# Order of three steps between the layers of an attention, SoLU and top-1 MoE kernel

## The chip, the core and the metric

The kernel runs on one core of a Trainium2 chip. The metric is the device time of one execution in microseconds (us). The core has five engines with queues of their own: TensorE (PE in the profile, its weight loads PEld), VectorE (DVE), ScalarE (ACT), GpSimd (POOL) and SyncE (SP), which only issues DMAs. POOL issues the indirect DMAs (gathers and scatters).

## The reference

3072 tokens (4 x 768) of width 512 pass through three layers:

```python
# chunked attention: chunks of 32 rows see 16 rows to the left, 8 to the right, 8 memory rows
scores = scale * np.matmul(q_c, k_full.transpose(0, 1, 3, 2))
a = np.exp(scores - max); a = a / (np.sum(a) + 1e-09)
x = np.matmul(a, v_full)
# SoLU with LayerNorm, 512 -> 1024 -> 512
h = x @ w_in
solu = h * softmax(h)
x = (solu - mu) / np.sqrt(var + 1e-06) * g_ln @ w_out
# top-1 mixture of 8 experts, 512 -> 1024 -> 512
e_idx = np.argmax(x @ w_gate, axis=1)
for e in range(E):
    h = np.maximum(x[mask] @ w1[e], 0.0)
    out[mask] = gate_w[mask, None] * eom[mask, e, None] * (h @ w2[e])
```

The result is float32. Products run in float16 with a high and a low half for each operand and three passes (high by high, high by low, low by high).

## The kernel before, in words

The first two layers and the routing go over 24 tiles of 128 tokens (NT = 24). Every step of a tile (a product, an exp, a transpose by DMA) is put down by `at(t, fn, ...)` with a planned time t. All are then sorted by t and emitted, and each engine works through its instructions in that order. The planned times are an order written out by hand; they hold nothing back by themselves. TL is the planned start of the last tile.

The routing of a tile (`routing_steps`) takes the logits on TensorE from x2T, the transposed second-layer output (line 350 is the helper of all three-pass products). VectorE makes lg, top, idx, the one-hot row oh_all and ng from them. `earlier` counts on TensorE the tokens ahead (tri and ones times oh_all), and VectorE makes the pick zz, the rank and the place (ohs, oav) from it. `slot_products` adds up the places of tiles 0 to 21 and later of the last two; `slot_numbers` makes the list of row numbers (slots_gidx) by which tokens are gathered. The rows themselves are kept in x2d in DRAM.

The third layer runs in nine units, a unit being a set of slots for tokens of one expert. Unit 0 has 384 slots of expert 1, unit 1 another 320 of the same expert, so with the same weights; units 2 to 8 have 480, 416, 352, 320, 320, 320 and 288 slots, one for each other expert, in the order of their counts. For a unit:
- `gather` (POOL, line 1238) fetches up to 128 rows each into a tile xg or x2; `slot_T` (SP, line 1250) transposes them by DMA into xu. Unit 1 has three such pieces (128, 128, 64), unit 2 four.
- `own_h(n, f)`, f = 0 to 7, is the first product, 12 matmuls into a PSUM tile pg (four buffers). `own_r` makes the two halves of its relu, ru: the high half on ScalarE (line 1261), the low half on VectorE (line 1262).
- `own_y` is the second product (line 1276), one piece of rows at a time, into one of two PSUM tiles. `slot_out` scales it on ScalarE (line 1333) and scatters it (POOL, line 1334). `strip_gates` (line 1314) copies gate factors of narrow pieces on VectorE.
- The weights of an expert come in two halves, w1 into wf0 and w2 into wf1, 2 MB each (`load_w`, SP, line 1221). `conv_hi` (ScalarE, line 1225) and `conv_lo` (VectorE, line 186) turn each into two float16 halves in four parts. `some(k)` emits up to k such conversions, if the target buffer has been used up, and after the fourth the load of the next set into the buffer that came free.

Unit 0's first product is spread over the last tiles, between the steps of their second layer and routing: f = 6 stands at TL + 33.4, f = 7 at TL + 35.5. The loop over units 1 to 8 stands behind the sorted steps and emits its calls in the order in which they are written. Lines 918, 1379, 1380 and 1458 are those that the change touches.

Of the kernel before, what the change touches and what calls it, by code (L numbers as in the profile page):

```python
# [38 lines left out]
def attention_solu_top1_moe(  # L39
# [30 lines left out]
    NT = N // P  # L70
# [7 lines left out]
    KF = DFF // P  # L78
# [256 lines left out]
    PERIOD = 14.2  # L335
# [5 lines left out]
    def at(t, fn, *args):  # L341
        events.append((t, len(events), fn, args))
# [211 lines left out]
    def when(name):  # L554
        return PLAN[name] - STEADY + 5 * PERIOD
# [160 lines left out]
    def routing_steps(i, v):  # L716
# [116 lines left out]

        at(LOGITS[i], logits)
        g = PICK[i]
# [79 lines left out]
    TL = (NT - 1) * PERIOD  # L915
    OUT = [(i + 2) * PERIOD + 6.15 for i in range(NT - 3)] + [TL + 5.3, TL + 14.6, TL + 24.0]
    X2 = [(i + 2) * PERIOD + 13.3 for i in range(NT - 4)] + [TL - 3.2] + [TL + 10.5, TL + 19.8, TL + 29.3]
    LOGITS = [(i + 3) * PERIOD + 12.8 for i in range(NT - 4)] + [TL + 12.4, TL + 19.8, TL + 29.2, TL + 33.3]
    PICK = [(i + 3) * PERIOD + 13.2 for i in range(NT - 4)] + [TL + 13.0, TL + 20.9, TL + 30.3, TL + 34.4]
    EARLIER = [(i + 4) * PERIOD + 6.1 for i in range(NT - 5)] + [TL + 10.3, TL + 14.2, TL + 21.9, TL + 31.3, TL + 35.45]  # L920
    GATE = [(i + 4) * PERIOD + 6.55 for i in range(NT - 5)] + [TL + 11.0, TL + 15.0, TL + 23.0, TL + 32.2, TL + 37.0]
    LOGITS[0:2] = [when("lg0"), when("lg1")]
    PICK[0:2] = [when("pk0"), when("pk1")]
# [181 lines left out]
    def left_over():  # L1105


        nc.vector.tensor_scalar(out=rt["ti"], in0=rt["all"], scalar1=float(P - 1), scalar2=None, op0=ALU.add)
        nc.vector.tensor_scalar(out=rt["ti"], in0=rt["ti"], scalar1=7, scalar2=None, op0=ALU.logical_shift_right)
        nc.vector.tensor_copy(rt["tr"], rt["ti"])  # L1110
        nc.vector.tensor_tensor(out=rt["tr"], in0=rt["tr"], in1=rt["room"][:, 2], op=ALU.subtract)
        nc.vector.tensor_tensor(out=rt["key"], in0=rt["all"], in1=rt["room"][:, 0], op=ALU.is_gt)
        nc.vector.tensor_tensor(out=rt["tr"], in0=rt["tr"], in1=rt["key"], op=ALU.mult)
        nc.vector.tensor_tensor(out=rt["tm"], in0=le_e, in1=rt["tr"].unsqueeze(1).to_broadcast([P, E, E]), op=ALU.mult)
        nc.vector.tensor_reduce(out=rt["ends"], in_=rt["tm"], axis=AX.X, op=ALU.add)
        nc.vector.tensor_copy(rt["ctl"][:, 2, 0:1], rt["ends"][:, E - 1:E])
# [56 lines left out]
    def cap(n):  # L1173
        return UNITS[n][1] if UNITS[n][0] == "own" else P

    def width(n):
        return -(-cap(n) // P)
# [5 lines left out]
    def pieces(n):  # L1183

        out_ = []
        for c in range(width(n)):
            m, row = rows(n, c), 0
            for size in (P, 64, 32):
                if m - row >= size:
                    out_.append((c, row, size))  # L1190
                    row += size
        return out_
# [10 lines left out]
    def weights(n):  # L1203

        return max(0, n - 1)

    def load_w(j, m, c=None, other=None):

        w, k = ((w1, KD), (w2, KF))[m]
        to = 0 if j == 0 else m  # L1210
        dst = wf[to].rearrange("p (k f) -> p k f", k=k)
        if j == 0:
            q = slice(c * k // 4, (c + 1) * k // 4)
            nc.sync.dma_start(out=dst[:, q], in_=w[FE].rearrange("(k p) f -> p k f", p=P)[:, q])
            return
        key = j if other is None else ("other", other)
        if key not in reg:
            at_ = rt["ctl"][0:1, 0, j - 1:j] if other is None else rt["ctl"][0:1, 1, other:other + 1]
            reg[key] = nc.values_load(at_, engines=[SP], min_val=0, max_val=E - 1)
        q = slice(0, k) if c is None else slice(c * k // 2, (c + 1) * k // 2)  # L1220
        nc.sync.dma_start(out=dst[:, q], in_=w[bass.ds(reg[key], 1)].rearrange("o (k p) f -> (o p) k f", p=P)[:, q])
# [31 lines left out]
    def own_h(n, f):  # L1253
        xt, wt = xT_t[n], hl[weights(n) % 2, 0].rearrange("p a (k f) -> p a k f", k=KD)
        ps = psum["g"].tile([P, HALF], F32, tag=f"g{f % 2}", name="pg")[:, 0:cap(n)]
        three(ps, [(wt[:, b_, kk, f * P:(f + 1) * P], xt[:, a * KD + kk]) for kk in range(KD) for a, b_ in PASSES])
        r_t[n, f] = ps

    def own_r(n, f):
        ps, r = r_t.pop((n, f)), rt["ru"]  # L1260
        nc.scalar.activation(out=r[:, 0, f, 0:cap(n)], in_=ps, func=AF.Relu)  # L1261
        nc.vector.scalar_tensor_tensor(  # L1262
            out=r[:, 1, f, 0:cap(n)], in0=ps, scalar=0.0, in1=r[:, 0, f, 0:cap(n)], op0=ALU.max, op1=ALU.subtract
        )
# [43 lines left out]
    def strip_gates(n):  # L1308

        for k, (c, row, m) in enumerate(pieces(n)):  # L1310
            if m < P:
                many = tiny(f"many{m}")
                for q in range(P // m):
                    nc.vector.tensor_copy(many[q * m:(q + 1) * m], xg_t[n, c].bitcast(F32)[row:row + m, DM:DM + 1])
                gate_of[n, (c, row, m)] = many

    def slot_out(n, piece):

        c, row, m = piece
        fold = P // m  # L1320
        dm = DM // fold
        y = ending.pop((n, piece), None)
        if y is None:
            y = lnp.tile([P, DFF], F32, tag="eh", name="eh")
        y = y[:, 0:dm]
        at_ = place(n, c, sidx)
        if fold > 1:
            col = BASES[n - 1] + c
            at_ = rt["split"][:, SPLITS.index((row, m)), col:col + 1]
            gate = gate_of.pop((n, piece))  # L1330
        else:
            gate = xg_t[n, c].bitcast(F32)[:, DM:DM + 1]
        nc.scalar.activation(out=y, in_=y_t.pop((n, piece))[:, 0:dm], func=AF.Copy, scale=gate)  # L1333
        put = nc.gpsimd.indirect_dma_start(  # L1334
            out=out if fold == 1 else out.rearrange("n (h d) -> (n h) d", h=fold),
            out_offset=bass.IndirectOffsetOnAxis(ap=at_, axis=0), in_=y, in_offset=None,
            bounds_check=N * fold - 1, oob_is_err=False,
        )
        for other in scattered:
            tc.declare_no_dep(put.ins, other.ins, reason="each token has one slot: scatters never share a row")  # L1340
        scattered.append(put)
# [34 lines left out]
        at(TL + 39.5 + 0.3 * c, gather, 1, c)  # L1376
        at(TL + 43.0 + 0.3 * c, slot_T, 1, c)
    for c in range(width(2)):
        at(TL + (41.0 if c < 2 else 50.8) + 0.3 * c, gather, 2, c)
        at(TL + (45.0 if c < 2 else 54.0) + 0.3 * c, slot_T, 2, c)  # L1380
    for c in range(4):
        at(TL + 41.6 + 1.2 * c, conv_hi, 1, 0, c)
        at(TL + 42.6 + 1.2 * c, conv_lo, 1, 0, c)
# [17 lines left out]
    def some(k=1):  # L1401
        for _ in range(k):
            if not parts or (parts[0][0] - 2, parts[0][1]) not in done:
                return
            j, m, c = parts.pop(0)
            conv_hi(j, m, c)
            conv_lo(j, m, c)
            if c == 3 and j + 1 < SETS:
                load_w(j + 1, m)

    def each(step, n):
        if n < RARE:
            for c in range(width(n)):
                step(n, c)
# [30 lines left out]
    for n in range(1, RARE):  # L1445
        todo = pieces(n)
        for f in range(KF):
            if n > 1 or f:
                own_h(n, f)
                own_r(n, f)  # L1450
            if f == 0 and n > 1:
                slot_out(*last)
                each(gather, n + 1)
            if f == 1 and 1 < n < RARE - 1:
                each(slot_T, n + 1)
            if f == 5 and n < RARE - 1:
                strip_gates(n + 1)
            if (2 if n == 1 else 0) < f < KF - 1:
                some()
            if n == 1 and f == 3:  # L1460
                load_w(2, 0)
            if n == 2 and f == 3:
                left_over()
        done.add((weights(n), 0))
        if n == RARE - 1:
            spare = psum["xu"].tile([P, 2 * KD, cap(n)], F16, tag="xu", name="xu").rearrange("p k t -> p (k t)").bitcast(F32)
            ending[n, todo[-2]], ending[n, todo[-1]] = spare[:, 0:DM], spare[:, DM:2 * DM]
        for k, piece in enumerate(todo):
            own_y(n, piece)
            if k and (n < RARE - 1 or k < len(todo) - 1):  # L1470
                slot_out(n, todo[k - 1])
            some(3)
        done.add((weights(n), 1))
        last = (n, todo[-1])
# [53 lines left out]
```

## Time and profile before

| | |
|---|---|
| median of 3 runs | 642.46 us (638.76 to 643.50) |
| the profiled execution, own time | 643.06 us |
| its span | 641.4 us |
| TensorE busy | 613.6 us (96%), 6955 matmuls |
| VectorE busy | 408.0 us (64%) |
| ScalarE busy | 310.7 us (48%) |
| POOL busy | 175.9 us (27%) |
| mean granted TensorE clock | 0.989 |

The profile is of one execution. The span goes from its first to its last instruction; the own time has 1.66 us more around it. An engine's busy time counts its instructions, not its waits; matmul ends are modelled. The granted clock is 1.00 at 2.4 GHz.

### The profile page before, as it was taken

The page shows a single profiled execution, that of the slowest core. Times are in us where ns is not written, and L with a number is a line of the kernel's source. Part 1 is how long each engine was busy: PE and PEld are TensorE (multiplying, and loading weights), DVE is VectorE, ACT ScalarE, POOL GpSimd, SP SyncE. Part 2 cuts the span into 40 slices and gives each one's busy share as a digit, 9 for nine tenths or more (in the row PEclk, how much of TensorE's full clock was granted, in tenths as well). Part 3 has the DMA queues.
Part 4 walks back from the last instruction along what each step waited for, and adds up shares of the span by engine and source line. Part 5 has one row for each costly group of instructions (what it writes and reads, how often), then busy time and mean ns, then how long its engine had stood idle before and what let it go on. Part 6 is the DMA issues. An engine that isn't in the chain of part 4 may idle for free.

```text
span 641.4 us, 17082 instructions
## 1 busy us (share of the span) xinstructions
PE 613.6 (96%) x6955; PEld 338.4 (53%) x6955; DVE 408.0 (64%) x1209; ACT 310.7 (48%) x648; POOL 175.9 (27%) x201
## 2 busy tenths in 40 slices
PE   9899899999999999999999989899999999999993
PEld 5555445555555555545554545454554656657561
DVE  3999866878889788878876662437153536365020
ACT  5667864565665566554444231445243436354120
POOL 2213342233332432233332124031221312313101
PEclk9999999999999999999999989999999999999997
DMA  8975879799999999966558359988546485794101
GB/s 269 344 241 113 185 182 171 165 198 230 239 189 208 193 240 219 181 138 123 123 109 171 90 179 204 300 304 226 190 114 254 124 285 148 276 185 130 37 8 40
DMA packets 168262, 117.44 MB, mean 183 GB/s; under 512 B 125724, under 2 KB 149678, under 8 KB 167664
## 3 DMA queue, kind: packets, MB, share of 16 engines
q1 hardware_dynamic: 162096, 96.94, 64.2%
q0 software_dynamic: 6080, 19.34, 9.9%
q8 instruction: 56, 0.92, 0.6%
q14 instruction: 30, 0.25, 0.1%
HBM read 73.69 MB, written 12.94 MB: 135 GB/s over the span
## 4 chain that ended last, share of the span: by engine, by line
PE 29%; issue 26%; DVE 21%; DMA 8%; POOL 7%; ACT 7%; SPq 1%; POOLq 0%; ACTq 0%; DVEq 0%
PE h L582 10%; PE pt L350 7%; PE pg L350 4%; DMA out_dram<-eh,split 3%; POOL out_dram L1334 3%; POOL xg L1238 3%; DVE nm L592 3%; PE warm L909 2%; ACT eh L600 2%; DVE eh L604 2%; DMA wf<-in_moe_w_dram 2%; PE pt L1276 2%; PE sc L367 1%; DVE mx L381 1%; DVE x L186 1%
## 5 line engine op out<-in xcount | busy, mean ns | idle before, releaser
L582 PE MATMUL h<-win_hl,xT 128*128 128x512 f16 x576 | 131.7, 379 | 2.9 <-DVE eh L604 1.4
L350 PE MATMUL pt<-wout_hl,lnT 128*128 128x512 f16 x552 | 129.2, 379 | 1.2 <-DVE x L186 1.1
L1262 DVE SCALAR_TENSOR_TENSOR ru<-pg,ru 128x320 f16<-128x320 f32 (+5 forms) x72 | 37.8, 525 | 112.1 <-ACT ru L1261 112.0
L1276 PEld LDWEIGHTS <-ru 128*128 128x128 f16 (+2 forms) x1176 | 70.0, 101 | 66.3 <-issue 6.0
L582 PEld LDWEIGHTS <-xT 128*128 128x128 f16 x576 | 53.1, 98 | 63.7 <-issue 2.5
L350 PEld LDWEIGHTS <-lnT 128*128 128x128 f16 x576 | 53.2, 97 | 57.4 <-issue 1.5
L350 PE MATMUL pg<-xu,hl 128*128 128x320 f16 (+2 forms) x480 | 75.2, 317 | 2.1 <-DMA xu<-x 1.2
L1276 PE MATMUL pt<-hl,ru 128*128 128x512 f16 (+2 forms) x528 | 74.9, 325 | 2.4 <-DVE ru L1262 2.4
L1261 ACT ACTIVATE ru<-pg 128x320 f16<-128x320 f32 (+5 forms) x72 | 33.5, 466 | 83.1 <-PE pg L350 82.0
L648 POOL TENSOR_TENSOR lnhl<-eh,lnhl 128x1024 f16<-128x1024 f32 x23 | 49.5, 2152 | 77.8 <-ACT lnhl L644 64.6
L350 PEld LDWEIGHTS <-hl 128*128 128x128 f16 x480 | 46.5, 99 | 27.2 <-DMA xu<-xg 2.7
L1276 PE MATMUL pt<-wout_hl,ru 128*32 128x128 f16 (+2 forms) x648 | 59.9, 285 | 0.0
L350 PE MATMUL pg<-xu,win_hl 128*128 128x480 f16 (+3 forms) x384 | 59.3, 316 | 0.0
L1334 POOL DMA_INDIRECT out_dram<-eh,slots_sidx x17 | 17.6, 1037 | 148.7 <-ACT eh L1333 148.7
L350 PEld LDWEIGHTS <-win_hl 128*128 128x128 f16 x384 | 37.2, 98 | 21.3 <-issue 0.6
L600 ACT ACTIVATE eh<-h,nm 128x1024 f32<-128x1024 f32 x24 | 26.8, 1115 | 41.9 <-DVE zr L793 35.0
L419 POOL TENSOR_TENSOR e<-e,sm 128x512 f32<-128x512 f32 x24 | 28.7, 1197 | 62.7 <-DVE sm L416 45.8
L186 DVE SCALAR_TENSOR_TENSOR hl<-wf,hl 128x1024 f16<-128x1024 f32 x32 | 38.6, 1224 | 7.9 <-ACT hl L1225 7.5
L1225 ACT ACTIVATE hl<-wf 128x1024 f16<-128x1024 f32 x32 | 32.9, 1047 | 3.0 <-DMA wf<-in_moe_w_dram 3.0
L604 DVE SCALAR_TENSOR_TENSOR eh<-h,eh 128x1024 f32<-128x1024 f32 x24 | 29.4, 1223 | 6.3 <-ACT eh L600 6.3
L909 PE MATMUL warm<-wide 128*128 128x384 f16 x169 | 31.4, 345 | 1.4 <-DVE mhalf L156 1.4
L621 ACT ACTIVATE junk<-eh,su 128x1024 f16<-128x1024 f32 x24 | 27.7, 1153 | 9.5 <-DVE pr L616 7.8
(193 smaller groups left out, 833.9 us busy)
## 6 DMA issues: line engine op xcount, KB each, us to landing
wf<-in_moe_w_dram SPq DMA_DIRECT2D x14, 2048.0 KB
vw<-in_v_dram SPq DMA_DIRECT2D x96, 112.0 KB
kr<-in_k_dram SPq DMA_DIRECT2D x12, 560.0 KB
qt<-in_q_dram SPq DMA_DIRECT2D x12, 512.0 KB
x2d<-x POOLq DMA_DIRECT2D x23, 260.0 KB, 3.7
wd<-in_moe_w_in_dram SPq DMA_DIRECT2D x4, 1024.0 KB
wd<-in_moe_w_out_dram SPq DMA_DIRECT2D x4, 1024.0 KB
wf<-in_moe_w_dram SPq DMA_DIRECT2D x8, 512.0 KB
```

The source lines that it names most:

```text
L186: nc.vector.scalar_tensor_tensor(out=lo, in0=src, scalar=s, in1=hi, op0=ALU.mult, op1=ALU.subtract)
L350: nc.tensor.matmul(out=out_ap, lhsT=a, rhs=b_, start=(z == 0), stop=(z == n - 1))
L582: nc.tensor.matmul(out=v["h"][:, n * HALF:(n + 1) * HALF], lhsT=xt[:, a * KD + kk], rhs=win_hl[:, b_, kk, n * HALF:(n + 1) * HALF], start= ...
L600: nc.scalar.activation(out=v["e"], in_=v["h"], func=AF.Exp, bias=v["nm"], scale=IH, accum_out=v["se"])
L604: nc.vector.scalar_tensor_tensor(out=e, in0=v["h"], scalar=IH, in1=e, op0=ALU.mult, op1=ALU.mult, accum_out=v["su"])
L648: eng.tensor_tensor(out=v["ln"][:, 1], in0=v["e"], in1=v["ln"][:, 0], op=ALU.subtract)
L909: nc.tensor.matmul(out=t[:, 0:3 * P], lhsT=wide[:, 0:P], rhs=wide, start=True, stop=True)
L1225: nc.scalar.activation(out=hl[b, m][:, 0, cs], in_=wf[m if of is None else of][:, cs], func=AF.Copy, scale=(S_W1, S_W2)[m])
L1261: nc.scalar.activation(out=r[:, 0, f, 0:cap(n)], in_=ps, func=AF.Relu)
L1262: nc.vector.scalar_tensor_tensor(out=r[:, 1, f, 0:cap(n)], in0=ps, scalar=0.0, in1=r[:, 0, f, 0:cap(n)], op0=ALU.max, op1=ALU.subtract)
L1276: nc.tensor.matmul(out=y_t[n, piece][q * m:(q + 1) * m, 0:DM // fold], lhsT=r[:, a, kk, at_:at_ + m], rhs=wt[:, b_, kk, q * DM // fold:(q ...
L1334: put = nc.gpsimd.indirect_dma_start(out=out if fold == 1 else out.rearrange("n (h d) -> (n h) d", h=fold), out_offset=bass.IndirectOffset ...
```

## The change

Three places in the order of emission change; what is computed stays.

1. The logits of the last tile are put down at TL + 33.5 in place of 33.3, so behind unit 0's product f = 6 (TL + 33.4).
2. The gathers and transposes of unit 2's first two pieces are put down with those of its other two, so behind the scatter of unit 0's second piece on POOL and behind the load of unit 2's second matrix (`load_w, 1, 1`, at TL + 52.4) on SP.
3. In unit 1's first product the four calls of `some()` at f = 3 to 6 are left out. The conversions follow with the calls of `some(3)` behind each piece of unit 1's second product. For units 2 to 8 the new condition says the same as the old one.

```diff
-    LOGITS = [...] + [TL + 12.4, TL + 19.8, TL + 29.2, TL + 33.3]
+    LOGITS = [...] + [TL + 12.4, TL + 19.8, TL + 29.2, TL + 33.5]
...
     for c in range(width(2)):
-        at(TL + (41.0 if c < 2 else 50.8) + 0.3 * c, gather, 2, c)
-        at(TL + (45.0 if c < 2 else 54.0) + 0.3 * c, slot_T, 2, c)
+        at(TL + 50.8 + 0.3 * c, gather, 2, c)
+        at(TL + 54.0 + 0.3 * c, slot_T, 2, c)
...
             if f == 5 and n < RARE - 1:
                 strip_gates(n + 1)
-            if (2 if n == 1 else 0) < f < KF - 1:
+            if n > 1 and 0 < f < KF - 1:
                 some()
             if n == 1 and f == 3:
                 load_w(2, 0)
```

On TensorE before, at the end of unit 0's product f = 5 (hl00 is the weight half, pg_6089 its PSUM tile, x2T_6063 the last tile's transposed input of the logits):

```order
3580 L350 MATMUL pg_6089<-xu_5666,hl00_1148 128x384
3581 L350 LDWEIGHTS hl00_1148
3582 L350 MATMUL pg_6089<-xu_5666,hl00_1148 128x384
3583 L350 LDWEIGHTS x2T_6063
3584 L350 MATMUL pg_6133<-wg_hl_115,x2T_6063 128x16
3585 L350 LDWEIGHTS x2T_6063
```

On TensorE after, 24 rows further on, where product f = 6 (pg_6136) ends:

```order
3604 L350 MATMUL pg_6136<-xu_5666,hl00_1148 128x384
3605 L350 LDWEIGHTS hl00_1148
3606 L350 MATMUL pg_6136<-xu_5666,hl00_1148 128x384
3607 L350 LDWEIGHTS x2T_6063
3608 L350 MATMUL pg_6149<-wg_hl_115,x2T_6063 128x16
3609 L350 LDWEIGHTS x2T_6063
```

The 24 rows of the logits and the 24 of product f = 6 have changed places; behind both, the slot products (oav) follow from row 3631 as before.

On ScalarE before, from the relu of f = 2 of unit 1 (ru 128x320) to the first output of unit 1's second product (eh_6622; wout_hl is the half of unit 2's second matrix, hl00 that of unit 3's first):

```order
336 L1261 ACTIVATE ru_5499<-pg_6463 128x320 [waits PE_49]
337 L1225 ACTIVATE wout_hl_114<-wf1_5498 128x1024 [waits DMAHW5_49]
338 L1261 ACTIVATE ru_5499<-pg_6491 128x320 [waits PE_49]
339 L1225 ACTIVATE wout_hl_114<-wf1_5498 128x1024
340 L1261 ACTIVATE ru_5499<-pg_6508 128x320 [waits PE_49]
341 L1225 ACTIVATE wout_hl_114<-wf1_5498 128x1024
342 L1261 ACTIVATE ru_5499<-pg_6533 128x320 [waits PE_49]
343 L1225 ACTIVATE wout_hl_114<-wf1_5498 128x1024
344 L1261 ACTIVATE ru_5499<-pg_6551 128x320 [waits DVE_49,PE_49]
345 L1225 ACTIVATE hl00_1148<-wf0_1147 128x1024 [waits DMAHW0_49]
346 L1225 ACTIVATE hl00_1148<-wf0_1147 128x1024 x2
347 L1333 ACTIVATE eh_6622<-pt_6566,xg_6308 128x512 [waits DMASW1_49,DMASW3_49,PE_49,Activation_49]
```

On ScalarE after, from the relu of f = 4 of unit 1 on (eh_6613 and eh_6674 are the outputs of its first and second piece):

```order
337 L1261 ACTIVATE ru_5499<-pg_6489 128x320 [waits PE_49]
338 L1261 ACTIVATE ru_5499<-pg_6504 128x320 [waits PE_49]
339 L1261 ACTIVATE ru_5499<-pg_6527 128x320 [waits PE_49]
340 L1261 ACTIVATE ru_5499<-pg_6542 128x320 [waits DVE_49,PE_49]
341 L1225 ACTIVATE wout_hl_114<-wf1_5498 128x1024 [waits DMAHW3_49]
342 L1225 ACTIVATE wout_hl_114<-wf1_5498 128x1024 x2
343 L1333 ACTIVATE eh_6613<-pt_6557,xg_6308 128x512 [waits DMASW3_49,DMASW7_49,PE_49,Activation_49]
344 L1225 ACTIVATE wout_hl_114<-wf1_5498 128x1024
345 L1225 ACTIVATE hl00_1148<-wf0_1147 128x1024 [waits DMAHW0_49]
346 L1225 ACTIVATE hl00_1148<-wf0_1147 128x1024
347 L1333 ACTIVATE eh_6674<-pt_6588,xg_6310 128x512 [waits DMASW4_49,PE_49,Activation_49]
348 L1225 ACTIVATE hl00_1148<-wf0_1147 128x1024 x2
```

The first conversion, with its wait for the load (DMAHW), stood ahead of the relus of f = 4 to 7 and now stands behind all eight relus.

On SP before, from unit 1's third transpose on (xu_6346 is unit 1's, xu_6357 unit 2's; DMASW is a wait for a gather):

```order
229 L1250 DMA_TRANSPOSE xu_6346<-x2_6312 128x8x64 [waits DMASW5_49]
230 L1250 DMA_TRANSPOSE xu_6357<-x2_6314 128x8x128 [waits DMAHW3_49,DMASW6_49,PE_49]
231 L1250 DMA_TRANSPOSE xu_6357<-x2_6316 128x8x128 [waits DMAHW4_49,DMASW7_49]
232 L1221 ISA
233 L1221 DMA wf1_5498<-in_moe2_w2_dram 128x8x512 [waits DMAHW5_49]
234 L1250 DMA_TRANSPOSE xu_6357<-xg_6406 128x8x128 [waits DMAHW6_49,DMASW2_49]
235 L1250 DMA_TRANSPOSE xu_6357<-xg_6408 128x8x96 [waits DMAHW7_49,DMASW3_49]
```

On SP after (xu_6342 is unit 1's, xu_6428 unit 2's):

```order
229 L1250 DMA_TRANSPOSE xu_6342<-x2_6312 128x8x64 [waits DMASW5_49]
230 L1221 ISA
231 L1221 DMA wf1_5498<-in_moe2_w2_dram 128x8x512 [waits DMAHW3_49]
232 L1250 DMA_TRANSPOSE xu_6428<-x2_6399 128x8x128 [waits DMAHW4_49,DMASW0_49,PE_49]
233 L1250 DMA_TRANSPOSE xu_6428<-x2_6401 128x8x128 [waits DMAHW5_49,DMASW1_49]
234 L1250 DMA_TRANSPOSE xu_6428<-xg_6403 128x8x128 [waits DMAHW6_49,DMASW2_49]
235 L1250 DMA_TRANSPOSE xu_6428<-xg_6405 128x8x96 [waits DMAHW7_49,DMASW3_49]
```

The load of wf1 has moved ahead of unit 2's first two transposes, and all four of them now follow it.

## Rows read from the trace of the kernel before

**Rows 1.** Stretches: us, busy us of PE, PEld, DVE, ACT, POOL; clock, DMA share, GB/s.

```profile
371.00:375.00 4.00, 4.00 (x30) 2.11 (x31) 1.01 (x7) 0.00 (x0) 0.00 (x0) 0.57 0.89 343
411.20:416.00 4.80, 2.40 (x11) 0.57 (x10) 4.61 (x12) 1.76 (x5) 0.00 (x0) 0.99 0.86 341
416.00:419.80 3.80, 3.80 (x11) 1.37 (x12) 2.85 (x3) 3.80 (x5) 0.14 (x1) 0.56 0.64 220
425.86:630.60 204.74, 204.73 (x1682) 120.82 (x1680) 84.49 (x129) 82.04 (x125) 45.44 (x43) 1.00 0.54 164
```

**Rows 2.** Timeline of PE, 366 to 430 us: start, duration, instruction, idle time before.

```profile
367.07 2.11 PE L350 MATMUL pg<-xu,hl 128*128 128x384 f16 x12
370.95 0.46 PE L350 MATMUL pg<-wg_hl,x2T 128*128 128x16 f16 x12 [1.77 <-DMA x2T<-x]
371.27 3.75 PE L350 MATMUL pg<-xu,hl 128*128 128x384 f16 x12
374.82 0.75 PE L350 MATMUL pm<-ohs,oav 128*128 128x26 f16 x22
...
375.97 0.17 PE L350 MATMUL pg<-oh_all,tri 128*128 128x8 f16 x1
...
379.32 0.20 PE L350 MATMUL pm<-ohs,oav 128*128 128x26 f16 x2
...
379.42 14.40 PE L1276 MATMUL pt<-hl,ru 128*128 128x512 f16 x66
395.06 13.20 PE L350 MATMUL pg<-xu,hl 128*128 128x320 f16 x96 [1.23 <-DMA xu<-x]
408.10 4.66 PE L1276 MATMUL pt<-hl,ru 128*128 128x512 f16 x20
414.44 0.82 PE L1276 MATMUL pt<-hl,ru 128*128 128x512 f16 x3 [1.68 <-DVE ru L1262]
415.97 9.96 PE L1276 MATMUL pt<-hl,ru 128*128 128x512 f16 x73 [0.71 <-DVE ru L1262]
425.86 4.43 PE L350 MATMUL pg<-xu,win_hl 128*128 128x480 f16 x21
```

**Rows 3.** Timeline of ACT in unit 1's first product.

```profile
401.77 0.44 ACT L1261 ACTIVATE ru<-pg 128x320 f16<-128x320 f32 x1 [1.19 <-PE pg L350]
407.63 1.06 ACT L1225 ACTIVATE wout_hl<-wf 128x1024 f16<-128x1024 f32 x1 [5.41 <-DMA wf<-in_moe_w_dram]
```

**Rows 4.** Timeline of SP's queue: unit 1's third transpose, the load, unit 2's third transpose.

```profile
388.44 1.35 SPq L1250 DMA_TRANSPOSE xu<-x  x1
...
395.79 0.61 SPq L1221 DMA_DIRECT2D wf<-in_moe_w_dram  x1
...
399.73 4.36 SPq L1250 DMA_TRANSPOSE xu<-xg  x1
```

**Rows 5.** Chain of waits, 360 to 460 us: start, duration, what.

```profile
365.99 4.92 DMA x2T<-x
...
395.79 11.81 DMA wf<-in_moe_w_dram
```

**Rows 6.** Timeline of DVE in the routing of the last tile.

```profile
372.46 0.15 DVE L743 TENSOR_SCALAR ng<-top 128x1 f32<-128x1 f32 x1
375.58 0.56 DVE L1262 SCALAR_TENSOR_TENSOR ru<-pg,ru 128x384 f16<-128x384 f32 x1 [2.98 <-ACT ru L1261]
376.25 0.16 DVE L758 SCALAR_TENSOR_TENSOR zz<-oh_all,pg 128x8 f32<-128x8 f16 x1
...
378.40 0.34 DVE L820 TENSOR_SCALAR oav<-iota_p,col,part 128x128 f16<-128x128 f32 x1
```

**Rows 7.** Tile xg, 376 to 412 us: time of its gathers from issue to landing.

```profile
DMA to landing us min/median/max: 4.4/6.2/8.3
```

**Rows 8.** Timeline, 420 to 480 us: weight loads of unit 1's narrow last piece.

```profile
423.12 2.54 PEld L1276 LDWEIGHTS <-ru 128*64 128x64 f16 x48 [0.42 <-issue]
```

**Rows 9.** Timeline of POOL: unit 2's third gather, behind unit 0's second scatter.

```profile
391.46 0.99 POOL L1238 DMA_INDIRECT xg<-x2d,slots_gidx  x1 [0.30 <-issue]
```

More of the change, by code (lines that the diff above doesn't have):

```diff
@@ L917, in attention_solu_top1_moe @@
     X2 = [(i + 2) * PERIOD + 13.3 for i in range(NT - 4)] + [TL - 3.2] + [TL + 10.5, TL + 19.8, TL + 29.3]
-    LOGITS = [(i + 3) * PERIOD + 12.8 for i in range(NT - 4)] + [TL + 12.4, TL + 19.8, TL + 29.2, TL + 33.3]
+    LOGITS = [(i + 3) * PERIOD + 12.8 for i in range(NT - 4)] + [TL + 12.4, TL + 19.8, TL + 29.2, TL + 33.5]
     PICK = [(i + 3) * PERIOD + 13.2 for i in range(NT - 4)] + [TL + 13.0, TL + 20.9, TL + 30.3, TL + 34.4]
```

## Prediction

> **What bounds the kernel now.** I read the busy time by stages first. From unit 2's first product, at 425.86 us, to the last matmul, TensorE is busy for 204.73 of 204.74 us at full clock [rows 1]. Nothing waits there, so each us by which that point moves earlier goes to the end, one for one, if the weights still arrive in time. What can be won lies ahead of 425.86.
>
> So I went through TensorE's timeline ahead of it [rows 2] and found three places where it is idle or slow:
> - Last tile's logits. The fixed unit's product f = 5 starts at 367.07 and takes 2.11 us, so it ends at 369.18. The logits start at 370.95, after a wait on the transposed x2T. Product f = 6, the same 12 matmuls as f = 5, takes 3.75 us in place of 2.11: the clock was granted at 0.57 from 371 to 375 [rows 1]. The count of earlier tokens follows at 375.97, and the end of the slot products, which give the gathers their addresses, at 379.32.
> - Unit 1's start. Its first product begins at 395.06, 1.23 us after the engine came free, on a transpose into xu.
> - Unit 1's second product. It runs from 408.10 to 425.86, 17.76 us, with waits of 1.68 and 0.71 us on ru, VectorE's low half of the relu. TensorE is busy for 2.40 of the 4.80 us from 411.2 to 416, and then works at a clock of 0.56 until 419.8 [rows 1].
>
> The third place is explained on ScalarE [rows 3]: after the relu of f = 3 at 401.77 it stands until 407.63, where a weight conversion gets its load. The relus of f = 4 to 7 are queued behind the four conversions. The load is late because SyncE issues it at 395.79, behind two transposes of unit 2 that wait for their gathers [rows 4]; it lands 11.81 us later [rows 5].
>
> **The change part by part.** All times are of the profiled execution: span 641.4 us, own time 643.06; the median of the runs shown is 0.60 below that, and the runs lie 4.74 us apart.
>
> 1. *Logits behind f = 6.* Product f = 6 starts at 369.18 and, with no gap before it, I cost it as f = 5: 2.11 us, to 371.29. x2T has landed by then (370.91) [rows 5], so the logits wait for nothing: 371.29 instead of 370.95, 0.34 later. From the logits' start to the last of the routing operations that the count waits for (ng) it takes 372.46 + 0.15 - 370.95 = 1.66 us on VectorE [rows 2, 6]: 372.95. The 44 small slot products fill TensorE meanwhile (some 1.15 us of it, 374.82 to 375.97). The count then stands at about 373.05, in place of 375.97: 2.92 earlier. VectorE must fit too. The low half of f = 6's relu, 0.56 us, sits between ng and pick; before it waited for the slow product until 375.58. Now it runs from 372.95 to 373.51, pick follows, and the 2.49 us from pick (376.25) to the end of the last place operation (378.40 + 0.34) [rows 6] end at 376.0. The slot products' last part stands behind TensorE's own work at 379.32 - 2.92 = 376.4. So the gathers and TensorE both move by 2.9 us.
>
> 2. *Unit 2's first gathers and transposes behind.* The work that TensorE does next, 14.40 us from 379.42, is free of waits and ends at 390.9. Then unit 1 needs its third transpose. In the trace that was issued at 388.44 [rows 4] and released TensorE at 395.06, 6.6 us later, with two gathers and a transpose of unit 2 in the same time. Moved by 2.9 it would be issued at 385.5. Lower bound: it lands like x2T, 4.92 us after its issue [rows 5], at 390.5, and TensorE starts when free, 390.9. Upper bound within this mechanism: it keeps its 6.6 us, 392.1. Two gathers less stand beside it, a scatter and the load come beside it; I take 391.4.
>
> By the Trainium skill, page "DMA: Bandwidth & Descriptors", section "Queues, rings and completion order", each DMA engine takes the descriptors of one queue in ring order; so the load, issued behind the transposes, could not pass them, and the sum below would be 0.5 us less. The same section has the engines take turns between queues, by which POOL's gathers and the load slow each other; the trace agrees as far as gathers land in 4.4 to 8.3 us [rows 7].
>
> The load itself leaves right behind the third transpose, at 385.5 + 1.35 + 0.2 = 387.0 instead of 395.79, and with its 11.81 us lands at 398.8. The transposes of unit 2 stand behind it on SyncE; in the trace one such, issued into the running load, held the queue for 4.36 us instead of 1.35 [rows 4]. Their gathers come behind POOL's second scatter, where the third stood at 391.46, 2.9 earlier, at a step of 0.99 + 0.30 us [rows 9]: the first at 388.6, the fourth at 392.5. Landed after about 6 us [rows 7], from 394 on, four transposes at 4.36 end at 411.5, and the last has landed by 416.4. Unit 2 needs them at 417.6. That is hidden by little in this worst sum; at 1.35 once the load is through they are done by 405.
>
> 3. *No conversions beside unit 1's first product.* It runs as it did, 13.04 us (395.06 to 408.10): 391.4 to 404.4. The relus of f = 4 to 7 follow each product at once, so the second product finds all of ru. VectorE's six gate copies between f = 5 and 6 need unit 2's fourth gather, which at 8.3 us [rows 7] lands by 400.8; they come up at 402. The second product without stalls: two pieces of 24 matmuls at 14.40 / 66 = 218 ns, 10.47 us, and the narrow piece 425.86 - 423.12 = 2.74 [rows 2, 8]: 13.2 us for 17.76. It ends at 417.6.
>
> The eight conversions have not gone: at 1.06 us on ScalarE and a little more on VectorE they now stand beside the second product, about 8.5 and 10 us in 13.2. The output of piece 0 waits behind three of them (404.4 + 3.2 = 407.6, earlier than the piece is done, 409.6). PSUM holds two pieces, so it costs nothing unless the load comes after 410. Unit 2's matrix is needed only by its second product, 19 us later.
>
> **Sum.** 425.86 - 417.6 = 8.2 us, of which the logits give 2.9, the transposes 0.7 and unit 1's second product 4.6. 643.06 - 8.2 = 634.8; the median lies a little lower than this execution, and I predict 634.6. With both bounds of the transpose it is 634.3 to 635.6. Units 2 to 8 keep their order, and their loads move along with the conversions that free the buffers.
>
> **Rivals.**
> - *The load holds unit 1's transpose.* The load now leaves 8.8 us earlier, 0.2 us behind the third transpose of unit 1. If they share the engines, the transpose is done only with the load, at 398.8. TensorE then stands for 7.9 us and works on at half clock, as after the stops at 371 and 416: the second of these ran 3.8 us at 0.56, a loss of 1.7. The end of unit 1 is 398.8 + 13.04 + 13.2 + 1.7 = 426.7, 0.9 later than before: 643.9. It is slower than before from a landing at 397.9 on, and by over 1% from 404. For it: the 4.36 us of a transpose beside a load, and a load that took 11.81 us. Against it: those were issued after the load, these before. 5%.
> - *Only the conversions pay.* The clock stays low at f = 6, or the logits' chain is held on VectorE, so that part 1 gives nothing, and unit 1's wait stays: 4.6 us, 638.5. For it: VectorE's relu stands in the chain. Against it: f = 5 ran at full clock [rows 2], and f = 6 now follows it without a stop. 12%.
> - *The stall moves on.* Unit 2's transposes, or the copies that need its fourth gather, come late, and TensorE waits 2 to 4 us at 417.6 or in unit 1's second product, half of the gain: 637 to 639. For it: the worst sum above leaves 1.2 us. Against: it takes 4.36 for all four. 15%.
> - *The tail does not follow*: a later load becomes the bound. No load is waited for after 425.86, and the buffers come free by 3 to 8 us earlier. 3%.
>
> **How the numbers follow.** My forecast has 65%. The runs before lie between 638.76 and 643.50, about 1% is what a measurement of this kernel can tell from no change, and 1% below the median is 636.0. Faster by over 1%: the forecast, and a little of the rivals with a low draw, less what scatters above 636.0: 0.68. Within 1%: 0.28. Slower by over 1%: 0.04. The range goes from 631.5 (both lower bounds and a run as far below the median as the lowest shown, part of the way) to 639.5 (the second and third rival).
>
> **What would show it.** Right: f = 6 takes 2.1 us and the logits wait for nothing; the count at about 373; unit 1 starts near 391.4; ScalarE does eight relus in a row; the second product has no wait on ru and takes 13.2 us; unit 2 starts near 417.6. Wrong: unit 1's start after 393, an idle stretch ahead of unit 2's first product, or new waits of TensorE after it.

## The result and the profile after

The changed kernel takes 637.15 us (median of 16 runs, 635.69 to 642.01), the kernel before 643.34 in the same comparison (16 runs, 638.76 to 646.65): 0.9905 of the time, 95% interval [0.9884, 0.9927], or 6.2 us less. Forecast were 634.6. The profiled execution of after took 635.88 us (span 634.2, clock 0.995), that of before 643.06 (641.4, 0.989).

In what follows I count from the start of the fixed unit's product f = 5. Where it falls (367.07 in before, 366.83 in after) is set by what comes earlier; it varied from 364.8 to 368.3 us in the thirteen profiles, so a difference of less than 3.5 us between the spans of two single profiles says nothing of the change by itself.

After's windows (us, then busy us and instructions of PE, PEld, DVE, ACT, POOL; clock, DMA share, GB/s). The first is that of [rows 1], the second is unit 1's second product, the third goes from unit 2's first product to the last matmul.

```profile
371.00:375.00 4.00, 3.92 (x70) 2.77 (x68) 3.50 (x28) 1.40 (x5) 0.00 (x0) 1.00 0.91 364
403.27:416.47 13.20, 13.20 (x99) 7.12 (x96) 6.07 (x6) 6.85 (x9) 1.00 (x1) 1.00 0.92 277
416.47:623.40 206.93, 205.77 (x1682) 121.12 (x1680) 88.18 (x133) 84.56 (x129) 46.97 (x44) 1.00 0.56 173
```

The half clock at 371 and at 416 has gone. But the third stretch, which was busy throughout in before, now holds 1.16 us of idle time.

After's timeline of PE, which answers to [rows 2] (... stands for small products between the rows):

```profile
366.83 4.06 PE L350 MATMUL pg<-xu,hl 128*128 128x384 f16 x24
370.73 0.45 PE L350 MATMUL pg<-wg_hl,x2T 128*128 128x16 f16 x12
...
372.36 0.17 PE L350 MATMUL pg<-oh_all,tri 128*128 128x8 f16 x1
...
375.71 0.20 PE L350 MATMUL pm<-ohs,oav 128*128 128x26 f16 x2
...
375.81 14.40 PE L1276 MATMUL pt<-hl,ru 128*128 128x512 f16 x66
390.24 13.20 PE L350 MATMUL pg<-xu,hl 128*128 128x320 f16 x96
403.27 13.27 PE L1276 MATMUL pt<-hl,ru 128*128 128x512 f16 x96
416.47 8.88 PE L350 MATMUL pg<-xu,win_hl 128*128 128x480 f16 x43
```

No row has a wait in brackets. f = 5 and f = 6 have become one row of 24 matmuls: 4.06 us, with no gap and at one speed. From f = 5's start to the end of the slot products it takes 8.88 us (375.71 - 366.83) where it took 12.25; unit 1 starts the moment the engine is free; its two products take 26.23 us (390.24 to 416.47) where they took 30.80. From f = 5 to unit 2 that is 49.64 in place of 58.79, 9.15 less.

After's timeline of ACT, for [rows 3]:

```profile
401.84 0.44 ACT L1261 ACTIVATE ru<-pg 128x320 f16<-128x320 f32 x1 [1.19 <-PE pg L350]
403.47 0.44 ACT L1261 ACTIVATE ru<-pg 128x320 f16<-128x320 f32 x1 [1.19 <-PE pg L350]
403.81 2.94 ACT L1225 ACTIVATE wout_hl<-wf 128x1024 f16<-128x1024 f32 x3
408.70 0.69 ACT L1333 ACTIVATE eh<-pt,xg 128x512 f32<-128x512 f32 x1 [1.96 <-issue]
409.29 1.05 ACT L1225 ACTIVATE wout_hl<-wf 128x1024 f16<-128x1024 f32 x1
414.52 2.00 ACT L1225 ACTIVATE hl<-wf 128x1024 f16<-128x1024 f32 x2 [4.19 <-DMA wf<-in_moe_w_dram]
```

The relus come at the products' pace, the conversions of the late load (wout_hl) right behind the last of them and without a wait: the load had landed. The output of piece 0 (L1333) stands ahead of the conversions of the next load, and it is those that wait now, for 4.19 us, with nothing urgent behind them.

After's SP queue, for [rows 4], and POOL's first gather:

```profile
373.79 0.36 SPq L789 DMA_DIRECT2D x2d<-x  x1
381.80 4.03 SPq L1250 DMA_TRANSPOSE xu<-xg  x2
386.52 1.19 SPq L1250 DMA_TRANSPOSE xu<-x  x1
387.91 0.79 SPq L1221 DMA_DIRECT2D wf<-in_moe_w_dram  x1
393.39 7.89 SPq L1250 DMA_TRANSPOSE xu<-x  x2
401.73 3.06 SPq L1250 DMA_TRANSPOSE xu<-xg  x2
```

```profile
378.46 1.02 POOL L1238 DMA_INDIRECT xg<-x2d,slots_gidx  x1 [9.02 <-DMA x2d<-x]
```

The load leaves right behind unit 1's third transpose, 21.1 us behind the start of f = 5 where it was 28.7; unit 2's transposes stand behind it, two of them at 3.9 us each, and the last is issued by 404.8, 11.7 us before it is needed. POOL's row has a new releaser: the first gather no longer waits for its addresses but for the gate that the last tile writes at 373.79. In before it was the addresses (slots_sidx):

```profile
380.53 1.82 POOL L1238 DMA_INDIRECT xg<-x2d,slots_gidx  x1 [10.84 <-DVE slots_sidx L1009]
```

After's timeline of PE in the second product of unit 2, from 440 us on:

```profile
439.81 16.24 PE L1276 MATMUL pt<-wout_hl,ru 128*128 128x512 f16 x189
456.52 0.34 PE L1276 MATMUL pt<-wout_hl,ru 128*32 128x128 f16 x9 [0.47 <-issue]
456.79 13.54 PE L350 MATMUL pg<-xu,hl 128*128 128x416 f16 x76
```

and in before, without a stop:

```profile
445.31 19.90 PE L1276 MATMUL pt<-wout_hl,ru 128*128 128x512 f16 x216
465.14 17.05 PE L350 MATMUL pg<-xu,hl 128*128 128x416 f16 x96
```

Here is most of the idle time of the third window: TensorE stops for 0.47 us in the piece of 32 rows and waits for nothing that the profile shows. Unit 4 has the same, 0.46 us at 520.72. Unit 2 takes 40.32 us (416.47 to 456.79) where it took 39.28 (425.86 to 465.14), so the stop and what goes with it cost 1.04. With unit 4's it is about 2 us, and that is why the profile pair differs by 9.4 us at unit 2's start and by 7.2 at the end.

### The profile page after: what moved, and what is told of

Read it like the earlier page. It is cut to its first block, busy times and chain, and to the rows that moved or that the text cites. A ratio compares the mean times of both kernels' runs of the same rounds, so it can differ in the third digit from the quotient of the medians.

```text
span 634.2 us, 17086 instructions
## 1 busy us (share of the span) xinstructions
PE 611.4 (96%) x6955; PEld 338.3 (53%) x6955; DVE 407.1 (64%) x1209; ACT 311.1 (49%) x648; POOL 175.9 (28%) x201
## 4 chain that ended last, share of the span: by engine, by line
PE 37%; issue 25%; DVE 18%; POOL 6%; ACT 6%; DMA 4%; SPq 2%; POOLq 0%; ACTq 0%; DVEq 0%
PE h L582 11%; PE pt L350 8%; PE pg L350 5%; PE pt L1276 5%; DMA out_dram<-eh,split 3%; POOL out_dram L1334 3%; PE warm L909 3%; DVE nm L592 2%; ACT eh L600 2%; POOL xg L1238 2%; PE sc L367 2%; DVE eh L604 2%; DVE mx L381 1%; PE xo L458 1%; DVE e L385 1%
## 5 line engine op out<-in xcount | busy, mean ns | idle before, releaser
L350 PE MATMUL pg<-xu,hl 128*128 128x320 f16 (+2 forms) x480 | 73.4, 312 | 0.7 <-ACT junk L621 0.6
L1261 ACT ACTIVATE ru<-pg 128x320 f16<-128x320 f32 (+5 forms) x72 | 33.5, 466 | 81.9 <-PE pg L350 80.0
L1276 PE MATMUL pt<-hl,ru 128*128 128x512 f16 (+2 forms) x528 | 72.8, 321 | 0.0
L350 PEld LDWEIGHTS <-win_hl 128*128 128x128 f16 x384 | 37.2, 98 | 21.5 <-issue 0.8
L419 POOL TENSOR_TENSOR e<-e,sm 128x512 f32<-128x512 f32 x24 | 28.7, 1197 | 62.1 <-DVE sm L416 45.0
```

The costliest lines, as they stand in the source:

```text
L350: nc.tensor.matmul(out=out_ap, lhsT=a, rhs=b_, start=(z == 0), stop=(z == n - 1))
L1276: nc.tensor.matmul(out=y_t[n, piece][q * m:(q + 1) * m, 0:DM // fold], lhsT=r[:, a, kk, at_:at_ + m], rhs=wt[:, b_, kk, q * DM // fold:(q ...
```

## Experiments

Two theories stood at the start. *A*: two of the parts cover the same loss. The relus stood because the load came late; part 2 (gathers and transposes behind the load) brings the load earlier, part 3 (no conversions beside unit 1's first product) takes the relus out from behind it, and either alone should do. *B*: part 3 is the one that does it, and part 2 moves a wait that costs nothing. About the tail, *E*: the narrow-piece stops come with the change of order; *D*: they come with the chip or the execution. The runs went to two chips, 13 (e1 to e4) and 12 (the others); that of the recorded pair is not on record.

Part 1 alone:

```diff
-    LOGITS = [...] + [TL + 12.4, TL + 19.8, TL + 29.2, TL + 33.3]
+    LOGITS = [...] + [TL + 12.4, TL + 19.8, TL + 29.2, TL + 33.5]
```

> Only the logits of the last tile move behind product f = 6. Both theories: f = 6 takes 2.1 us instead of 3.75, the count and the gathers come 2.9 us earlier, and nothing else changes its shape: unit 1 still waits some 1.2 us for its third transpose (start near 392.1) and its second product still takes 17 to 18 us. Unit 2 starts near 423.0 (2.9 earlier than the 425.86 of before). Time: 2.9 us less than before, ratio 0.995.

Part 2 alone:

```diff
-        at(TL + (41.0 if c < 2 else 50.8) + 0.3 * c, gather, 2, c)
-        at(TL + (45.0 if c < 2 else 54.0) + 0.3 * c, slot_T, 2, c)
+        at(TL + 50.8 + 0.3 * c, gather, 2, c)
+        at(TL + 54.0 + 0.3 * c, slot_T, 2, c)
```

> Only unit 2's first two gathers and transposes move behind the load. Theory A (either cover will do: the stall of unit 1's second product is the late load, and the load is late because SyncE holds it behind unit 2's transposes): the load leaves near 390, lands near 402, the conversions in unit 1's first product wait about 1 us instead of 5.4, the relus keep up, the second product takes 13.2 to 13.6 us and unit 2 starts 5 to 6 us earlier, near 420. Ratio 0.991. Theory B (the prediction's own split: this part is worth 0.7 us, and the 4.6 us hang on the conversions beside the product): unit 2 starts near 425.2, the second product still takes over 16 us. Ratio 0.999.

Part 3 alone:

```diff
-            if (2 if n == 1 else 0) < f < KF - 1:
+            if n > 1 and 0 < f < KF - 1:
```

> Only the conversions beside unit 1's first product are left out there. Both theories: unit 1 starts at 395.06 as before, the load still leaves near 395.8 and lands near 407.6, the eight relus run without a wait, the second product takes 13.2 us, and unit 2 starts near 421.3, 4.6 earlier. Ratio 0.993. If the conversions' late start costs something (theory C: ScalarE with eight conversions holds the outputs and PSUM), the second product takes 14 us or more.

Parts 1 and 2 without 3 (both of the first two diffs):

> The change without its part 3: logits and gathers moved, the conversions still beside unit 1's first product. Theory A: the load lands before the conversions are due (near 399 to 401 with unit 1's first product from 390 to 403), so part 3 adds nothing: the second product takes 13.2 to 13.6 us and unit 2 starts near 416.5 to 417, as in the change. Ratio to before 0.990, same as the change. Theory B: the second product still stalls by 3 us or more, unit 2 starts near 420 or later, ratio 0.995.

Then the kernel before and the change once more, each in a single execution:

> The kernel before, unchanged, for a second profile. In the profile of the change and of the four parts TensorE stops twice for about 0.5 us (put down to issue, not to a wait) in the pieces of 32 rows of units 2 and 4, and from unit 2's start to the end of the span it takes 217.7 to 218.0 us; the first profile of before had no such stop and 215.5 us. Theory D (the stops come and go from execution to execution, and the first profile was without them by chance): the second profile has them, 217.7 us. Theory E (the change of order causes them): no stops, 215.5 us again.

> The changed kernel, for a second profile. Mechanism as found: product f = 6 at 2.1 us, no wait of TensorE from unit 1's start to unit 2's, 26.2 us between them; from the count (the first small matmul of the last-but-one tile's count) to unit 2's start within 1 us of the first profile. Theory D: the stops in the narrow pieces may be there or not, and the span is 634.2 or some 2 us less; theory E: they are there.

The other two pairs, parts 1 and 3 and parts 2 and 3:

> The change without its part 2: logits moved, conversions left out beside unit 1's first product, unit 2's first gathers and transposes where they were. The load then leaves near 392 and lands near 404 to 406, while unit 1's first product, from about 391.5 on after a wait of 1 us, ends near 404.5: the conversions wait 1 us at most and hold nothing. Theory A (either cover will do, once the logits are moved): the second product takes 13.2 us, unit 2 starts 1 to 1.5 us later than in the change, ratio 0.992. Theory F (the load's time grows with what stands beside it, 14.5 us instead of 11.8 as with the logits alone): the conversions wait until 406, the first output piece leaves at 410 instead of 409, still no stall of TensorE; same time.

> The change without its part 1: gathers moved and conversions left out, logits ahead of f = 6 as before. TensorE waits for x2T again (1 to 3 us) and f = 6 may run at half clock; from unit 1's start on it is as in the change (26.2 us to unit 2's start, no wait). Unit 2 starts 2 to 3 us later than in the change, counted from the end of f = 5. Ratio to before 0.994 to 0.995.

Since part 2 looked idle, the change and parts 1 and 3 were timed side by side:

> The changed kernel, timed beside the next one on one chip. Ratio to before 0.990 to 0.993. TensorE from unit 1's start to unit 2's: 26.2 us, no wait. If the stops of 0.5 us in the narrow pieces belong to the chip (all four profiles of one chip had them, all four of another had none), every profile of this call has them or none has, these three alike.

> The change without its part 2, timed. Theory G (with the conversions out of unit 1's first product, the place of unit 2's gathers decides only the wait at unit 1's start, 0 to 1.2 us either way): ratio to before within 0.002 of the change's, second product of unit 1 13.2 us. Theory H (part 2 helps by the 0.7 us of the prediction or more): ratio 0.001 to 0.003 above the change's, and a wait of about 1 us at unit 1's start.

And one step further than the change, the load ahead of unit 1's transposes:

```diff
-    at(TL + 52.4, load_w, 1, 1)
+    at(TL + 42.9, load_w, 1, 1)
```

> The change, with the load of unit 2's second matrix put ahead of unit 1's three transposes on SyncE as well (issued near 374 instead of 388, behind the load of the first matrix that lands near 377.5). It tests the rival in which the load holds unit 1's transposes. If transposes wait for a load that was issued ahead of them on the same queue: the load runs until 384 to 388, unit 1's transposes, issued from 382 on, and the gathers beside it come late, and unit 1 starts 2 to 5 us later than in the change, ratio 0.994 to 0.998. If they share the engines and little is lost: unit 1 starts within 1.2 us of the change, ratio as the change.

What was measured. The last three columns are from each one's profile, in us: f = 5's start to the end of the slot products; unit 1's start to unit 2's; f = 5's start to unit 2's.

| kernel | median (runs) | before beside it | ratio [95%] | to slots' end | unit 1 | f = 5 to unit 2 |
|---|---|---|---|---|---|---|
| before | | | | 12.25 | 30.80 | 58.79 |
| before again, e5 | 636.31 (1) | 639.63 | single run | 10.52 | 27.92 | 54.26 |
| part 1, e1 | 641.45 (10) | 642.39 | 0.9984 [0.9957, 1.0011] | 8.88 | 34.03 | 58.56 |
| part 2, e2 | 641.71 (10) | 642.39 | 0.9993 [0.9969, 1.0016] | 10.40 | 29.29 | 54.04 |
| part 3, e3 | 639.10 (10) | 642.39 | 0.9951 [0.9924, 0.9977] | 13.19 | 26.24 | 54.68 |
| 1 and 2, e4 | 639.39 (10) | 642.39 | 0.9972 [0.9945, 0.9999] | 10.17 | 29.23 | 53.74 |
| 1 and 3, e7 | 634.52 (4) | 639.63 | 0.9896 [0.9834, 0.9958] | 8.88 | 26.24 | 49.83 |
| 1 and 3, e10 | 635.03 (7) | 638.90 | 0.9946 [0.9922, 0.9971] | 8.88 | 26.24 | 49.46 |
| 2 and 3, e8 | 635.81 (10) | 639.63 | 0.9940 [0.9908, 0.9973] | 14.17 | 26.24 | 54.75 |
| change | 637.15 (16) | 643.34 | 0.9905 [0.9884, 0.9927] | 8.88 | 26.23 | 49.64 |
| change again, e6 | 634.66 (1) | 639.63 | single run | 8.88 | 26.23 | 50.74 |
| change again, e9 | 634.78 (6) | 638.90 | 0.9919 [0.9890, 0.9949] | 8.87 | 26.24 | 49.72 |
| load ahead, e11 | 637.85 (10) | 638.90 | 0.9999 [0.9973, 1.0026] | 10.04 | 26.23 | 52.08 |

The ratio is not the quotient of the two medians beside it; the two differ by up to 0.0024 (e7: 0.9896, and 0.9920 by the medians), which is 1.5 us. And a profile is one execution, not always a middling one: e2's and e10's were the fastest of their runs, e8's the slowest.

**Part 3 decides unit 1's length.** In all eight profiles that have it, with or without the other two, the column says 26.23 or 26.24, the figure worked out for it in the prediction. Without it, the five values lie between 27.92 and 34.03. With part 3 alone (e3) the second product has no wait, and takes the 13.2 us that leave no room for theory C:

```profile
394.32 13.20 PE L350 MATMUL pg<-xu,hl 128*128 128x320 f16 x96 [0.75 <-DMA xu<-x]
407.36 13.26 PE L1276 MATMUL pt<-hl,ru 128*128 128x512 f16 x96
```

It is also the only part that, timed alone, is clear of no change (0.9951). Theory A falls: part 2 shortened the stall and did not end it. The timeline of PE in e2:

```profile
403.41 5.14 PE L1276 MATMUL pt<-hl,ru 128*128 128x512 f16 x23
409.26 5.57 PE L1276 MATMUL pt<-hl,ru 128*128 128x512 f16 x25 [0.71 <-DVE ru L1262]
416.92 2.81 PE L1276 MATMUL pt<-hl,ru 128*64 128x256 f16 x48 [2.08 <-ACT eh L1333]
```

that of the load on SP's queue:

```profile
387.15 0.43 SPq L1221 DMA_DIRECT2D wf<-in_moe_w_dram  x1
```

and that of ACT:

```profile
400.92 1.06 ACT L1225 ACTIVATE wout_hl<-wf 128x1024 f16<-128x1024 f32 x1 [3.39 <-DMA wf<-in_moe_w_dram]
...
413.34 2.95 ACT L1225 ACTIVATE hl<-wf 128x1024 f16<-128x1024 f32 x3 [7.22 <-DMA wf<-in_moe_w_dram]
416.20 0.67 ACT L1333 ACTIVATE eh<-pt,xg 128x512 f32<-128x512 f32 x1
```

With the load 7.2 us earlier, counted from f = 5 (21.5 us behind it, in before 28.7), the relu wait is down to 0.71. But the four conversions and the relus are then done by 406.1, and the conversions for the next unit come up early: three of them, waiting for a load of their own, stand ahead of piece 0's output. PSUM holds two pieces, so the third piece waits 2.08 us for that output; in e4, 2.42. In after the same conversions stand behind the output (ACT's rows above). So part 3 helps in two ways, of which the prediction had the first. Theory B had the division of the work right. That e2 reached unit 2 at 419.66, near theory A's 420 and far from B's 425.2, is luck of the execution for the most part: of the 6.2 us against before, 1.5 are an earlier f = 5, 1.9 a fast f = 6, and unit 1 itself has 1.5. Timed, e2 gave 0.9993, B's figure and not A's 0.991.

**Part 1 works on a wait that differs from execution to execution.** Of the eight profiles with part 1, the six in which x2T landed before it was wanted all take 8.87 or 8.88 us to the slots' end. The other two, e4 and e11, waited 1.11 and 0.99 us for x2T and took 10.17 and 10.04. Without part 1 it is 10.40 to 14.17. Two of those, e5 and then e8:

```profile
368.59 0.46 PE L350 MATMUL pg<-wg_hl,x2T 128*128 128x16 f16 x12 [1.69 <-DMA x2T<-x]
368.90 2.11 PE L350 MATMUL pg<-xu,hl 128*128 128x384 f16 x12
```

```profile
372.27 0.49 PE L350 MATMUL pg<-wg_hl,x2T 128*128 128x16 f16 x12 [3.08 <-DMA x2T<-x]
372.61 4.00 PE L350 MATMUL pg<-xu,hl 128*128 128x384 f16 x12
```

e5 is before's kernel once more: it waits 1.69 us and f = 6 then runs at full speed; in before it waited 1.77 and f = 6 took 3.75 [rows 2]. Against 8.88, the five without part 1 lose 1.5 to 5.3 us; against the two in which x2T came late even with part 1, 0.2 to 4.1. Before's profile was one of the three in which f = 6 was slow as well: the clock in it was 0.54, in e3 0.60 and in e8 0.50, in e2 and e5 1.00.

Alone, part 1 gains nothing at unit 2. The SP queue of e1:

```profile
391.46 0.75 SPq L1221 DMA_DIRECT2D wf<-in_moe_w_dram  x1
```

its ACT:

```profile
405.97 1.06 ACT L1225 ACTIVATE wout_hl<-wf 128x1024 f16<-128x1024 f32 x1 [8.61 <-DMA wf<-in_moe_w_dram]
```

and its PE:

```profile
390.20 13.20 PE L350 MATMUL pg<-xu,hl 128*128 128x320 f16 x96 [1.15 <-DMA xu<-x]
403.24 2.75 PE L1276 MATMUL pt<-hl,ru 128*128 128x512 f16 x12
407.40 0.61 PE L1276 MATMUL pt<-hl,ru 128*128 128x512 f16 x2 [1.41 <-ACT ru L1261]
...
414.30 10.00 PE L1276 MATMUL pt<-hl,ru 128*128 128x512 f16 x73 [0.71 <-DVE ru L1262]
424.23 4.02 PE L350 MATMUL pg<-xu,win_hl 128*128 128x480 f16 x19
```

Unit 1 started earlier, but the load took 14.5 us from its issue, the relus stood for 8.61, and unit 1 took 34.03: 3.2 of the 3.4 us came back as stall. The expectation (17 to 18 us for the second product) missed that; it took 20.99. With part 3 there, part 1's gain reaches unit 2: 49.46 to 50.74 us with it, 54.68 and 54.75 without (e3, e8, with waits of 3.12 and 3.08 us on x2T). The times show less: the pair without part 1 (e8) stands at 0.9940, the change on the same chip at 0.9919, and the intervals overlap. So what part 1 is worth is read from profiles, and is not shown by time.

**Part 2 gives nothing that these runs can tell, once part 3 is there.** e7 and e10 reach unit 2 in 49.83 and 49.46 us, the change in 49.64, 50.74 and 49.72; timed on one chip the medians differ by 0.25 us (e9, e10). The ratios differ by 0.0027, which theory H had named as the price of leaving part 2 out (0.001 to 0.003), but the intervals overlap, and the same kernel as e10 had 0.9896 in e7, below the change's. The wait at unit 1's start, which it was to shorten, was 0.20 and 0 us without it (e7, e10), and 0, 1.12 and 0 with it (after, e6, e9); the wait of 1 us that belongs to H is not there. So neither G nor H is shown.

**The narrow-piece stops come with the chip or the execution (D).** They are in all four profiles of chip 13, in e2 too, whose order on TensorE is before's, and in after's first profile; in none of the seven of chip 12, e6 and e9 with the whole change among them. The same place in e6:

```profile
436.90 19.90 PE L1276 MATMUL pt<-wout_hl,ru 128*128 128x512 f16 x216
```

So E falls. Whether it is the chip or the execution isn't shown, and why they come wasn't found.

**The load ahead of the transposes** takes the gain away by the ratio (0.9999; by the medians 1.05 of the 4.1 us are left). SP in e11:

```profile
375.66 0.39 SPq L1221 DMA_DIRECT2D wf<-in_moe_w_dram  x1
385.89 2.66 SPq L1250 DMA_TRANSPOSE xu<-xg  x2
388.64 7.20 SPq L1250 DMA_TRANSPOSE xu<-x  x3
```

and PE:

```profile
392.83 13.20 PE L350 MATMUL pg<-xu,hl 128*128 128x320 f16 x96 [1.30 <-DMA xu<-x]
```

From POOL's first gather (378.70) to the first transpose on SP it takes 7.19 us here, with the load running beside it; in after it is 3.34 (378.46 to 381.80), in e6 and e9 3.45 and 3.35. Other profiles without such a load have up to 5.32 (e3); in e4, where x2T came late as in e11, it is 5.10. So the gathers land some 2 to 4 us later, and TensorE waits 1.30 us for the third transpose, where the change had waited 0 to 1.12 (and e5, without such a load, 1.31). Unit 1 starts 1.3 to 2.4 us later than in the three profiles of the change, counted from f = 5; that lies between the two expectations, and the time is beyond both. Of the 52.08 us to unit 2, another 1.16 come from the late x2T, which a load issued after it can't have caused. The timed loss against the change is 3.1 us by the medians (637.85 to 634.78) and 5 by the ratios. The profile accounts for less than half of it, and the rest stays open; the profiled execution (636.50) was among the lower of ten (635.63 to 642.76).

The Trainium skill, page "DMA: Bandwidth & Descriptors", section "Queues, rings and completion order", has each DMA engine take turns between the queues that have work for it. The 2 to 4 us by which POOL's gathers came later beside SyncE's load agree with that; the turns themselves are in no row.

## Why the prediction was right, point by point

- *Each us at unit 2's start goes to the end.* Right in the seven profiles of chip 12, where it is 215.4 to 215.7 us from there to the end of the span, as in before (641.4 - 425.86 = 215.5); in the recorded pair 2.2 of 9.4 us stayed in the narrow-piece stops, which no row of before had shown.
- *How sure.* The likeliest of the three outcomes, faster by over 1% (0.68), is not what the median shows: it is 0.95% less, and the interval, 0.7 to 1.2%, holds both sides of that line.
- *Part 1, 2.9 us.* Right in kind, and mis-sized for the recorded pair: it measured 3.37 (12.25 - 8.88). f = 6 took 2.11 with no gap, and the logits waited for nothing. VectorE fitted. "The gathers and TensorE both move by 2.9" failed in its first half: counted from f = 5 the first gather moved by 1.8 us (380.53 - 367.07 = 13.46 in before, 378.46 - 366.83 = 11.63 in after), since the gate's write comes last now. In after it cost TensorE nothing.
- *Part 2, 0.7 us.* In the recorded profile the lower bound held: unit 1 started when TensorE came free, and its wait of 1.23 us went. But e6 waited 1.12 with part 2, so the bound holds in two of the change's three profiles; and e7 and e10 0.20 and 0 without it, so this can't be credited to part 2. The 1.21 us that the recorded pair gave here may be luck of the execution.
- *The load, 11.81 us.* Mis-sized where it can be seen: beside transposes and gathers the load took 13.8 us in e2 (387.15 to 400.92) and 14.5 in e1 (391.46 to 405.97). In after nothing waited for it, so its landing isn't shown, only that it was in by 403.8, when its conversions came up.
- *Part 3, 4.6 us.* Right: 4.57 (30.80 - 26.23), unit 1 at 26.23 against 26.24. But the stall that it removes is no constant: 1.68 us in e5, and 4.6 in before.
- *The sum, 8.2 us.* The recorded pair of profiles gave more up to unit 2: 3.37 at the logits, 1.21 at unit 1's start and 4.57 in unit 1, 9.15 together. The tail took 2.2 of it back, and the pair's own times differ by 7.2; the medians differ by 6.2, since after's execution was the second fastest of 16. So two misses of opposite sign stand behind the nearness of 7.2 to 8.2. On chip 12 the single profiles of before and after (e5, e6) differ by 3.5 us up to unit 2 (54.26 to 50.74), and the timed gain was 4.1 us by the medians (e9). That the stalls are smaller there in most executions would fit, but two profiles don't show it.
- *Rivals.* The load did not hold unit 1's transpose in the change; e11, which puts it ahead of the transposes, shows the load delaying them by way of the gathers, at a price of 1.30 us at most in the profile and not of 8. Nothing moved on into unit 2. "Only the conversions pay" would have been 4.6 us. It falls by the profiles, in which part 1 gives 3.37 us in the recorded pair; by time it is not ruled out: part 3 alone was timed at 3.3 us less than before (e3) and the pair without part 1 at 3.8 (e8), beside 4.1 for the change on e8's chip.

## What to carry to other kernels

Where several edits aim at one loss, ask first which of them takes the waiting instruction out of the in-order queue: here that one gave the same 26.23 or 26.24 us whenever the load left (8.7 us behind f = 5 in e11, 29.6 in e3), while bringing the load earlier only moved the place where the queue was blocked. One profile gives a stall as one execution had it; where it hangs on a DMA's landing, look at a second execution before its size goes into a sum. And count from a point just ahead of the change, since what came earlier varied by more than most of the parts gave.

## What was not expected of the hardware

- After waits of 1.57 and 1.69 us (e2, e5) the next product ran at full speed, 2.11 us; after 1.77 (before) it took 3.75, after 3.12 (e3) 3.32 and after 3.08 (e8) 4.00. The granted clock in these products was 1.00 in e2 and e5, 0.54 in before, 0.60 in e3 and 0.50 in e8, where 0.50 is the lower of the two levels (1.2 of 2.4 GHz); a mean between 0.50 and 1.00 says that it changed within the stretch. So a wait of about 1.7 us can cost itself alone, or as much again.
- The same instructions in the same order, a run of weight loads and matmuls of 32 rows, stop for some 0.46 us by the row ("issue") and cost about 1 us in the unit's length (1.04 in unit 2 of after), in all profiles of one chip and in after's first, and in none of another chip.
